# Channel attention with a squared-ReLU FFN: the folded weights of batches 1 to 3 by seven block products, and two steps of batch 0 in another order

## The chip, the cores and the metric

One core of a Trainium2 chip. The time is device microseconds of one launch; "before" is the median of 3 runs. The matrix engine TensorE is PE in the profile (PEld its weight loads), VectorE is DVE, ScalarE is ACT, and SP issues the DMAs.

## The reference

B = 4 batches of N = 6080 tokens with C = 256 channels; w_in is 256x2048, w_out 2048x256.

```
qn = q / (norm(q, axis=1) + 1e-06);  kn = k / (norm(k, axis=1) + 1e-06)
s = kn.transpose(0, 2, 1) @ qn / tau          # 256 x 256 per batch
a = softmax(s)                                # rows
x = v @ a
h = max(x @ w_in, 0)
out = (h * h) @ w_out
```

## The kernel before

v @ a @ w_in is computed as v @ W with W = a w_in, made once per batch: `e` is exp(s) (transposed: eT), `rinv` one over its row sums, and W(b, g) is group g of four, 512 columns of w_in each. Every operand of a product is split in two float32r parts, hi and lo, and a product is three terms: hi hi, hi lo, lo hi.

The tokens of a batch go in 12 blocks (ten of 512, the last two of 480). A **step** is one block and one f of 16 (128 columns of W). In a step PE makes `ps_h` = W v (`first_product`, six matmuls of a block's width), ACT puts relu of it into `x`. Two steps are a **pair**: ACT squares x, DVE makes the sums of the block products (`x<-x`, one op of 512 and two of 256 that depend on each other), ACT casts `g_hi`, DVE subtracts `g_lo`, once over three slots (768 columns) and once over four (1024). Two pairs later PE uses them in `second_product`, seven block products in place of eight, 9 matmuls of 256 in the even step and 12 in the odd (`seven_products`; the first two blocks use `eight_products`, six matmuls of 512 in each step). So in each step PE first makes ps_h, then ps_o, and the ps_o part needs g_hi and g_lo of a pair that ACT and DVE have had some four steps for.

PE, DVE and ACT run in the order in which the program is written; only SP's order is a scheduler's. Work beside the steps sits in generators: `beside` advances by one yield per step, and `attention(b)` (the Gram of q and k of the next batch, its norms, its softmax in `softmax_and_W`) runs beside the blocks of batch b-1. The norms are refined in three rounds of small DVE ops (nx, ny, ns, nu), end in `nr`, and ACT's `s<-gram,nr` waits for nr. At the end of `softmax_and_W` the four W(b, g) are made, in the last block of the batch before: g = 0 at f = 4 and 6, g = 1 at 9 and 11, g = 2 at 14 and the next block's 0, g = 3 at 5 and 7. Each is two halves h of six matmuls of 512 (`ps_w`), each followed a step later by an eviction: ACT writes w_hi (512), DVE w_lo (512, scalar_tensor_tensor from PSUM). The parts of w_in are kept in DRAM (`wi_kept`) and reloaded for each W(b, g).

Batch 0 differs: steps 0 to 31 go through its first two blocks in turn, while DVE and ACT still decode w_in and w_out (`decode`, the tiles dec_e, dec_m, w_raw) and split v (`split_v_hi`, `split_v_lo`). W(0, 1..3) are made in steps 6, 14 and 22 (`steps_of_W`).

Of the kernel before, what the change touches and what calls it, by code (L numbers as in the profile page):

```python
# [8 lines left out]
F32 = mybir.dt.float32  # L9
F32R = mybir.dt.float32r  # L10
# [3 lines left out]
AF = mybir.ActivationFunctionType  # L14
ALU = mybir.AluOpType
# [15 lines left out]
def kernel(  # L31
# [208 lines left out]
    QK_BUFS = 2  # L240
# [134 lines left out]
    def attention(b):  # L375

        if b not in grams:
            grams[b] = Gram(b)
        g = grams[b]
        c0 = HEAD if b == 1 else 0  # L380
        for c in range(c0, min(c0 + QK_BUFS, g.n)):
            g.load(c)
        yield
        for c in range(c0, g.n):
            yield from until_even()
            p, jn, _ = g.q[c]
            hi = pool.tile([P, 2, J, C], F32R, tag="qk_hi", name=f"qk_hi{b}_{c}", bufs=1)
            lo = pool.tile([P, 2, J, C], F32R, tag="qk_lo", name=f"qk_lo{b}_{c}", bufs=1)
            h_, l_, r_ = (x[:p, :, :jn, :] for x in (hi, lo, g.raws[c]))
            scalar.copy(h_, r_)  # L390
            vector.tensor_sub(l_, r_, h_.bitcast(F32))
            yield
            yield from until_even()
            g.squares(c)
            g.add_squares(c)
            if c + QK_BUFS < g.n:
                g.load(c + QK_BUFS)
            for _ in g.products(c, [(hi, hi), (hi, lo), (lo, hi)]):
                yield
        yield from softmax_and_W(b)  # L400

    def pause(b, first, other):

        for _ in range(other if b else first):
            yield

    def softmax_and_W(b):
        gram, acc = grams[b].gram, grams[b].acc
        wi = {0: reload_w_in(b, 0)} if b else {}

        vector.tensor_add(acc[:, :, 0, :], acc[:, :, 0, :], acc[:, :, 1, :])
        yield from pause(b, 1, 2)
# [1 line left out]
        for m in range(2 * NC):  # L414
# [4 lines left out]
                start=m == 0,  # L419
# [5 lines left out]
        x = small("nx")  # L425
# [59 lines left out]
        vector.tensor_copy(eT_hi, ps_tv)  # L485
        vector.tensor_sub(eT_lo, ps_tv, eT_hi.bitcast(F32))
        yield from pause(b, 2, 3)

        for g in range(NG):
            while (b, g) not in may_write_W:  # L490
                yield
            if b == 0:
                while g not in wi_first:
                    yield
                hi, lo = wi_first.pop(g)
                keep_w_in(g, (hi, lo))
# [31 lines left out]

            if b == 0:
                for h, terms in ((0, (0, 1)), (1, (0,)), (0, (2,)), (1, (1, 2))):  # L530
                    products(h, terms)
                yield
                for h in range(NC):
                    evict(h)
            else:
                for h in range(NC):
                    products(h)
                    if h == NC - 1 and g + 1 < NG:
                        wi[g + 1] = reload_w_in(b, g + 1)
                    yield  # L540
                    evict(h)
                    yield
# [291 lines left out]
    for i in range(len(steps) + 2 * LAG):  # L834
        part = now["part"] = i % 2
        if i < len(steps):
            b, n, f = steps[i]
            at = b * NB + n
            first_product(b, n, f)
            if n == NB - 1 and f % FPG == FPG - 1:  # L840
                may_write_W.add((b + 1, f // FPG))

        if i >= PAIR:
            gens = (beside,)
        else:
# [67 lines left out]
```

## Time and profile before

| | |
|---|---|
| median of 3 runs | 2214.52 us (2214.35 to 2214.86) |
| profiled execution | 2215.23 us, span 2213.5 us |
| busy: PE, ACT, DVE | 2205.0, 1847.7, 1774.4 us |
| granted TensorE clock | 1.0 |

PE is busy from end to end, so the time is the sum of PE's matmul pitches plus what PE waits. The durations of PE's rows are longer than the pitch, because a matmul starts before the one ahead of it has ended: what a matmul costs is the distance of starts.

### The profile page before, as it was taken

Reading aid. Unit: us, or ns where it says so; the run is one execution under the profiler, and the core shown is the slowest. Engines: PE = TensorE matmul, PEld = TensorE weight load, DVE = VectorE, ACT = ScalarE, POOL = GpSimd, SP = SyncE. Lnnn points to the kernel's source line nnn. Section 1 sums busy time; section 2 is a strip of 40 time slices with the busy share of each in tenths; the row PEclk is TensorE's granted clock in tenths of the full one; section 3 lists DMA queues with packets and bytes.
Section 4 is the critical chain, followed back from the end, with each engine's and each line's share of the span. In section 5 each row is a group of like instructions: output and inputs, shape, how many; then the busy total and the mean of one; then the engine's idle time right before and its main releaser. Section 6 shows DMA issues by size and latency. Waiting matters only on the chain.

```text
span 2213.5 us, 34513 instructions
## 1 busy us (share of the span) xinstructions
PE 2205.0 (100%) x13795; PEld 1982.1 (90%) x13795; DVE 1774.4 (80%) x2496; ACT 1847.7 (83%) x2300; POOL 0.7 (0%) x6
## 2 busy tenths in 40 slices
PE   9999999999999999999999999999999999999999
PEld 8788999989989999988998999998899888888898
DVE  6878888888778888878767888887877777787786
ACT  5788888888788888888878888888887888888887
POOL 0000000000000000000000000000000000000000
PEclk9999999999999999999999999999999999999999
DMA  9521122101121122110121222110102010010000
GB/s 340 181 77 38 60 74 68 46 19 38 57 67 58 61 69 65 61 41 22 36 76 48 63 68 72 58 53 22 35 23 76 21 37 20 22 36 20 21 27 18
DMA packets 76496, 127.01 MB, mean 57 GB/s; under 512 B 7728, under 2 KB 35120, under 8 KB 76336
## 3 DMA queue, kind: packets, MB, share of 16 engines
q1 hardware_dynamic: 76336, 124.81, 17.4%
q8 instruction: 108, 1.77, 0.3%
q14 instruction: 52, 0.43, 0.1%
HBM read 95.68 MB, written 29.10 MB: 56 GB/s over the span
## 4 chain that ended last, share of the span: by engine, by line
PE 96%; DMA 2%; DVE 1%; ACT 1%; SPq 0%; issue 0%; DVEq 0%; ACTq 0%
PE ps_h L27 47%; PE ps_o L27 42%; PE gram L27 4%; PE ps_w L27 2%; DMA qk<-in_k 1%; DMA qk<-in_q 0%; DVE dec_m L27 0%; DMA qk_heads<-in_q 0%; DMA w_raw<-in_w_in 0%; ACT x L27 0%; ACT g_hi L27 0%; SPq L268 0%; SPq L267 0%; DVE g_lo L27 0%; DVE wi_lo L27 0%
## 5 line engine op out<-in xcount | busy, mean ns | idle before, releaser
L27 DVE TENSOR_TENSOR g_lo<-x,g_hi 128x768 fp32r<-128x768 f32 (+2 forms) x749 | 808.8, 1080 | 78.9 <-ACT g_hi L27 78.2
L27 DVE TENSOR_TENSOR x<-x 128x512 f32<-128x512 f32 (+1 forms) x1095 | 558.4, 510 | 279.5 <-ACT x L27 253.8
L27 ACT CAST g_hi<-x 128x768 fp32r<-128x768 f32 (+2 forms) x749 | 701.8, 937 | 25.3 <-DVE x L27 12.3
L27 ACT ACTIVATE x<-ps_h 128x512 f32<-128x512 f32 (+1 forms) x768 | 455.8, 593 | 282.2 <-PE ps_h L27 264.1
L27 PE MATMUL ps_h<-v_hi,w_hi 128*128 128x512 f32 (+1 forms) x1536 | 478.4, 393 | 0.0
L27 PE MATMUL ps_h<-v_hi,w_lo 128*128 128x512 f32 (+1 forms) x1536 | 477.9, 392 | 0.0
L27 PE MATMUL ps_h<-v_lo,w_hi 128*128 128x512 f32 (+1 forms) x1536 | 475.0, 390 | 0.7 <-DVE v_lo L27 0.7
L27 ACT ACTIVATE x<-x 128x1024 f32<-128x1024 f32 (+1 forms) x384 | 404.5, 1053 | 11.9
L27 PE MATMUL ps_o<-g_lo,wS_hi 128*128 128x256 f32 (+1 forms) x1460 | 407.4, 279 | 0.0
L27 PE MATMUL ps_o<-g_hi,wS_lo 128*128 128x256 f32 (+1 forms) x1460 | 406.6, 279 | 0.0
L27 PE MATMUL ps_o<-g_hi,wS_hi 128*128 128x256 f32 (+1 forms) x1460 | 405.9, 278 | 0.0
L27 PEld LDWEIGHTS ps_h<-v_lo,w_hi 128*128 128x128 f32 x1536 | 287.8, 187 | 65.9 <-DVE v_lo L27 1.2
L27 PEld LDWEIGHTS ps_h<-v_hi,w_lo 128*128 128x128 f32 x1536 | 288.5, 188 | 62.4 <-DVE w_lo L27 0.3
L27 PE MATMUL ps_o<-g_hi,wo_hi 128*128 128x256 f32 (+2 forms) x1159 | 325.2, 285 | 0.0
L27 PE MATMUL ps_o<-g_hi,wo_lo 128*128 128x256 f32 (+2 forms) x1159 | 325.1, 285 | 0.0
L27 PE MATMUL ps_o<-g_lo,wo_hi 128*128 128x256 f32 (+2 forms) x1159 | 324.9, 285 | 0.0
L27 PEld LDWEIGHTS ps_o<-g_lo,wS_hi 128*128 128x128 f32 x1460 | 274.8, 188 | 16.1 <-DVE g_lo L27 0.2
L27 PEld LDWEIGHTS ps_o<-g_hi,wS_hi 128*128 128x128 f32 x1460 | 274.1, 188 | 15.6
L27 PEld LDWEIGHTS ps_o<-g_hi,wS_lo 128*128 128x128 f32 x1460 | 274.4, 188 | 0.0
L27 PEld LDWEIGHTS ps_h<-v_hi,w_hi 128*128 128x128 f32 x1536 | 238.2, 188 | 4.7
L27 PEld LDWEIGHTS ps_o<-g_hi,wo_hi 128*128 128x128 f32 x1159 | 218.4, 188 | 15.6
L27 PEld LDWEIGHTS ps_o<-g_lo,wo_hi 128*128 128x128 f32 x1159 | 217.7, 188 | 15.7 <-DVE g_lo L27 0.3
(96 smaller groups left out, 1689.2 us busy)
## 6 DMA issues: line engine op xcount, KB each, us to landing
qk<-in_k SPq DMA_DIRECT2D x87, 256.0 KB, 2.7
qk<-in_q SPq DMA_DIRECT2D x87, 256.0 KB, 3.0
v<-in_vT SPq DMA_DIRECT2D x40, 512.0 KB, 3.7
out_T<-o SPq DMA_DIRECT2D x152, 128.0 KB, 1.7
wi_hi<-wi_kept SPq DMA_DIRECT2D x12, 512.0 KB, 3.3
wi_lo<-wi_kept SPq DMA_DIRECT2D x12, 512.0 KB, 4.1
w_raw<-in_w_in SPq DMA_DIRECT2D x4, 1024.0 KB, 6.1
w_raw<-in_w_out SPq DMA_DIRECT2D x4, 1024.0 KB, 5.3
```

The costliest lines, as they stand in the source:

```text
L27: return lambda *args, **kwargs: self.tc.keep_in_program_order(issue(*args, **kwargs))
```

## The change

**W of batches 1 to 3.** The two halves by two halves of the product e w_in, twelve matmuls of 512, become seven block products of three terms, 21 matmuls of 256. Four go first (12 matmuls, into `one`, the bank of the Gram, and `two`, a ps_h buffer); ACT copies 256 columns, DVE makes three sums of 256 that depend on each other and adds one of them onto `two` (512 columns); two yields later the other three (9 matmuls), the first of S4 with B22, into `two`. The eviction is four pieces of 256 on ACT and on DVE, in place of two of 512. It stands in the yields where the second half's stood.

**Sums.** T1 to T4, sums of blocks of w_in, are made once, beside batch 1's softmax: `beside_another` lets `sums_of_w_in` go on in two of every five yields. For each g DVE adds hi and lo (1024), makes the sums (512, 256, 256) and subtracts the cast (1024); ACT casts (1024). They are stored in DRAM (`wS_kept`) and reloaded for each W(b, g). S1 to S4, sums of blocks of e, are made in each batch: DVE 512, four of 128 and 512, ACT 512.

**Batch 0.** In step 1 `split_v_lo` of block 1 stands ahead of the weights' stages. In steps 6, 14, 22 the last four matmuls of W, those with wi_lo, and the eviction stand behind that step's second product.

```
+    def sums_of_w_in(b, wi):
...
+            vector.tensor_add(w, hi.bitcast(F32), lo.bitcast(F32))
+            wi[(g + 1) % NG] = reload_w_in(b, (g + 1) % NG)
+            yield
...
+            vector.tensor_sub(S[:, 0:3:2, :], w[:, :, half:], w[:, 0, :].rearrange("p (k t) -> p k t", k=2))
+            vector.tensor_sub(S[:, 1, :], w[:, 1, half:], S[:, 0, :])
+            vector.tensor_sub(S[:, 3, :], w[:, 1, 0:half], S[:, 1, :])
+            yield
+            parts = wi_sums_tiles(b, 0, f"made{g}")
+            scalar.copy(parts[0], S)
+            yield
+            vector.tensor_sub(parts[1], S, parts[0].bitcast(F32))
+            for kept, part in zip(wS_kept[g], parts):
+                nc.sync.dma_start(kept, part.bitcast(F32))
+            yield
+        sums_made.append(b)
...
+        for k, _ in enumerate(main):
+            if k % 5 in (0, 2):
+                next(side, None)
+            yield
...
+            vector.tensor_add(e32, eT_hi.bitcast(F32), eT_lo.bitcast(F32))
...
+            vector.tensor_add(S[:, 0], A21, A22)
+            vector.tensor_sub(S[:, 2], A11, A21)
+            vector.tensor_sub(S[:, 1], S[:, 0], A11)
+            vector.tensor_sub(S[:, 3], A12, S[:, 1])
...
+            while not sums_made:
+                yield
+            wS = {g: reload_sums(b, g) for g in range(2)}
...
+                early = ((0, (0, 1)), (1, (0,)), (0, (2,)), (1, (1, 2))) if g == 0 else ((0, (0, 1)), (1, (0, 1)))
...
+                if g:
+                    for h in range(NC):
+                        products(h, (2,))
                 for h in range(NC):
                     evict(h)
             else:
-                for h in range(NC):
-                    products(h)
...
+                product(one[:, 0], "A11", "B11", start=True)
+                product(one[:, 1], "S2", "T2", stop=True)
+                product(two[:, 0], "S1", "T1", start=True)
+                product(two[:, 1], "S3", "T3")
+                scalar.copy(x[:, 0], one[:, 0])
+                vector.tensor_add(x[:, 1], one[:, 1], x[:, 0])
+                vector.tensor_add(x[:, 2], two[:, 0], x[:, 1])
+                vector.tensor_add(x[:, 3], two[:, 1], x[:, 2])
+                vector.tensor_add(two, two, x[:, 1:2, :].broadcast_to([P, 2, half]))
+                yield
+                yield
+                product(one[:, 0], "A12", "B21", stop=True)
+                product(two[:, 0], "S4", "B22")
+                product(two[:, 1], "A22", "T4", stop=True)
...
             for item in stages.get(i, ()):
                 weights.stage(item)
-            if i == 1:
-                split_v_lo(*order[1])
...
-        if i in steps_of_W:
-            next(first)
...
         if i >= 2 * LAG:
             second_product(*pairs[i // 2 - LAG], part)
+        if i in steps_of_W:
+            next(first)
```

DVE in block 11 of batch 0, while W(1, 0) is evicted and W(1, 1) made; before (behind g_lo and x stand block and pair, behind ps_w group and half):

```order
L27 TENSOR_TENSOR v_lo_0_5542<-v_0_5116,v_hi_0_5488 128x1024 [waits DMAHW1_49]
L27 TENSOR_TENSOR x_11_4_5529<-x_11_4_5529 128x480 [waits Activation_49]
L27 TENSOR_TENSOR x_11_4_5529<-x_11_4_5529 128x240 [waits DVE_49] x2
L27 TENSOR_TENSOR g_lo_11_4_5555<-x_11_4_5529,g_hi_11_4_5554 128x720 [waits Activation_49]
L27 TENSOR_TENSOR o_10_5364<-o_10_5364 128x240
L27 TENSOR_TENSOR o_10_5364<-o_10_5364 128x2x240 [waits DVE_49]
L27 SCALAR_TENSOR_TENSOR w_lo_1_5581<-ps_w_1_0_5582,rinv_4678,w_hi_1_5580 128x512 [waits Activation_49]
L27 TENSOR_TENSOR g_lo_11_4_5555<-x_11_4_5529,g_hi_11_4_5554 128x960 [waits Activation_49]
```

The same stretch now:

```order
L27 TENSOR_TENSOR v_lo_0_5654<-v_0_5191,v_hi_0_5594 128x1024 [waits DMAHW4_49]
L27 TENSOR_TENSOR x_11_4_5641<-x_11_4_5641 128x480 [waits Activation_49]
L27 TENSOR_TENSOR x_11_4_5641<-x_11_4_5641 128x240 [waits DVE_49] x2
L27 TENSOR_TENSOR g_lo_11_4_5667<-x_11_4_5641,g_hi_11_4_5666 128x720 [waits Activation_49]
L27 TENSOR_TENSOR o_10_5453<-o_10_5453 128x240
L27 TENSOR_TENSOR o_10_5453<-o_10_5453 128x2x240 [waits DVE_49]
L27 TENSOR_TENSOR w_sums_1_5696<-ps_w_1_0_5694,w_sums_1_5696 128x256 [waits Activation_49]
L27 TENSOR_TENSOR w_sums_1_5696<-ps_w_1_1_5695,w_sums_1_5696 128x256 [waits DVE_49,PE_49]
L27 TENSOR_TENSOR w_sums_1_5696<-ps_w_1_1_5695,w_sums_1_5696 128x256 [waits DVE_49]
L27 TENSOR_TENSOR ps_w_1_1_5695<-ps_w_1_1_5695,w_sums_1_5696 128x512 [waits DVE_49]
L27 TENSOR_TENSOR g_lo_11_4_5667<-x_11_4_5641,g_hi_11_4_5666 128x960 [waits Activation_49]
```

The w_lo of W(1, 1)'s first half has gone from here (it follows a pair on, with the second half's, as four of 256; just ahead of these rows the w_lo of W(1, 0), one of 512 before, is four of 256 too). In its place stand three sums that follow one another and the addition onto `two`.

PE at the end of step (11, 11), the second set of products of W(1, 1), now:

```order
L27 MATMUL ps_w_1_0_5694<-wi_lo_1_5576,eT_hi_4735 128x256
L27 MATMUL ps_w_1_0_5694<-wi_hi_1_5575,eT_lo_4736 128x256
L27 MATMUL ps_w_1_1_5695<-wi_hi_1_5575,eS_4900 128x256 [waits DVE_49]
L27 MATMUL ps_w_1_1_5695<-wi_lo_1_5576,eS_4900 128x256
L27 MATMUL ps_w_1_1_5695<-wi_hi_1_5575,eS_4900 128x256
L27 MATMUL ps_w_1_1_5695<-wiS_1_1_5390,eT_hi_4735 128x256
L27 MATMUL ps_w_1_1_5695<-wiS_1_1_5391,eT_hi_4735 128x256
L27 MATMUL ps_w_1_1_5695<-wiS_1_1_5390,eT_lo_4736 128x256
```

The third row, S4 with B22, waits for DVE; before, six matmuls of 512 stood here and had no row of DVE to wait for in their own group.

DVE in batch 1's norms, before:

```order
L27 SCALAR_TENSOR_TENSOR nu_4193<-ns_4192,ny_4189 128x4 [waits DVE_49]
L27 SCALAR_TENSOR_TENSOR ny_4189<-nu_4193,ny_4189 128x4 [waits DVE_49]
L27 TENSOR_TENSOR g_lo_8_2_4165<-x_8_2_4142,g_hi_8_2_4164 128x1024 [waits Activation_49]
L27 TENSOR_TENSOR x_8_3_4201<-x_8_3_4201 128x512 [waits Activation_49]
L27 TENSOR_TENSOR x_8_3_4201<-x_8_3_4201 128x256 [waits DVE_49] x2
L27 TENSOR_TENSOR g_lo_8_3_4228<-x_8_3_4201,g_hi_8_3_4227 128x768 [waits Activation_49]
L27 TENSOR_TENSOR o_7_4104<-o_7_4104 128x256
L27 TENSOR_TENSOR o_7_4104<-o_7_4104 128x256 [waits DVE_49]
L27 TENSOR_TENSOR ns_4192<-nx_4186,ny_4189 128x4
```

And now:

```order
L27 SCALAR_TENSOR_TENSOR nu_4207<-ns_4206,ny_4203 128x4 [waits DVE_49]
L27 SCALAR_TENSOR_TENSOR ny_4203<-nu_4207,ny_4203 128x4 [waits DVE_49]
L27 TENSOR_TENSOR wi_sums_4220<-wi_raw_4092 128x2x256
L27 TENSOR_TENSOR wi_sums_4220<-wi_raw_4092,wi_sums_4220 128x256 [waits DVE_49] x2
L27 TENSOR_TENSOR g_lo_8_2_4179<-x_8_2_4156,g_hi_8_2_4178 128x1024 [waits Activation_49]
L27 TENSOR_TENSOR x_8_3_4215<-x_8_3_4215 128x512 [waits Activation_49]
L27 TENSOR_TENSOR x_8_3_4215<-x_8_3_4215 128x256 [waits DVE_49] x2
L27 TENSOR_TENSOR g_lo_8_3_4246<-x_8_3_4215,g_hi_8_3_4245 128x768 [waits Activation_49]
L27 TENSOR_TENSOR o_7_4118<-o_7_4118 128x256
```

The sums of w_in, an op of 512 and two of 256, have come between the first round of the norms and g_lo; all that follows on DVE, the other rounds and nr among it, stands behind them.

## Rows read from the trace of the kernel before

**Rows 1.** The page's part 1 (busy time, share, instructions) and part 4 (the chain of work that ended last, by engine).

```profile
PE 2205.0 (100%) x13795; PEld 1982.1 (90%) x13795; DVE 1774.4 (80%) x2496; ACT 1847.7 (83%) x2300; POOL 0.7 (0%) x6
...
PE 96%; DMA 2%; DVE 1%; ACT 1%; SPq 0%; issue 0%; DVEq 0%; ACTq 0%
```

**Rows 2.** PE's timeline in a step away from W: start, duration, instruction, count. Six matmuls of 512, twelve of 256, and the next step's first.

```profile
1002.07 0.62 PE L27 MATMUL ps_h<-v_hi,w_hi 128*128 128x512 f32 x2
...
1003.46 0.28 PE L27 MATMUL ps_o<-g_hi,wS_hi 128*128 128x256 f32 x1
...
1004.86 0.63 PE L27 MATMUL ps_h<-v_hi,w_hi 128*128 128x512 f32 x2
```

**Rows 3.** PE's timeline in block 11 of batch 0: the first matmuls of the first half of W(1, 1) and of what follows it, and the same of the second half.

```profile
589.69 0.63 PE L27 MATMUL ps_w<-wi_hi,eT_hi 128*128 128x512 f32 x2
...
591.09 0.60 PE L27 MATMUL ps_h<-v_hi,w_hi 128*128 128x480 f32 x2
...
596.05 0.63 PE L27 MATMUL ps_w<-wi_hi,eT_hi 128*128 128x512 f32 x2
...
597.44 0.60 PE L27 MATMUL ps_h<-v_hi,w_hi 128*128 128x480 f32 x2
```

**Rows 4.** The page's part 5, PE's weight loads for ps_o: count, busy time, mean ns.

```profile
L27 PEld LDWEIGHTS ps_o<-g_lo,wS_hi 128*128 128x128 f32 x1460 | 274.8, 188 | 16.1 <-DVE g_lo L27 0.2
```

**Rows 5.** PE's timeline in step 6 of batch 0: W(0, 1), with what it waited for.

```profile
79.44 0.63 PE L27 MATMUL ps_w<-wi_hi,eT_hi 128*128 128x512 f32 x2
80.61 0.73 PE L27 MATMUL ps_w<-wi_lo,eT_hi 128*128 128x512 f32 x2 [0.54 <-DVE wi_lo L27]
81.18 0.63 PE L27 MATMUL ps_w<-wi_hi,eT_lo 128*128 128x512 f32 x2
```

**Rows 6.** DVE's timeline in the same stretch.

```profile
79.34 1.22 DVE L27 TENSOR_TENSOR wi_lo<-dec_m,wi_hi 128x1024 fp32r<-128x1024 f32 x1
```

**Rows 7.** PE's timeline in step 1 of batch 0 and the second product behind it.

```profile
70.09 0.73 PE L27 MATMUL ps_h<-v_lo,w_hi 128*128 128x512 f32 x2 [0.73 <-DVE v_lo L27]
...
73.80 0.72 PE L27 MATMUL ps_o<-g_lo,wo_hi 128*128 128x512 f32 x2
```

**Rows 8.** DVE's timeline of that stretch.

```profile
67.67 1.23 DVE L27 TENSOR_TENSOR wo_lo<-dec_m,wo_hi 128x1024 fp32r<-128x1024 f32 x1
68.82 1.22 DVE L27 TENSOR_TENSOR v_lo<-v,v_hi 128x1024 fp32r<-128x1024 f32 x1
...
72.52 1.23 DVE L27 TENSOR_TENSOR g_lo<-x,g_hi 128x1024 fp32r<-128x1024 f32 x1 [1.34 <-ACT g_hi L27]
```

**Rows 9.** ACT's timeline of that stretch.

```profile
66.58 1.06 ACT L27 CAST wo_hi<-dec_m 128x1024 fp32r<-128x1024 f32 x1 [1.24 <-DVE dec_m L27]
...
71.44 1.04 ACT L27 CAST g_hi<-x 128x1024 fp32r<-128x1024 f32 x1
```

**Rows 10.** DVE's timeline in block 11 of batch 0 (idle time and releaser in brackets).

```profile
585.22 1.55 DVE L27 TENSOR_TENSOR x<-x 128x480 f32<-128x480 f32 x3 [1.68 <-ACT x L27]
...
587.51 0.84 DVE L27 TENSOR_TENSOR o<-o 128x240 f32<-128x240 f32 x2
588.27 0.74 DVE L27 SCALAR_TENSOR_TENSOR w_lo<-ps_w,rinv,w_hi 128x512 fp32r<-128x512 f32 x1
...
594.41 0.74 DVE L27 SCALAR_TENSOR_TENSOR w_lo<-ps_w,rinv,w_hi 128x512 fp32r<-128x512 f32 x1
595.08 1.15 DVE L27 TENSOR_TENSOR g_lo<-x,g_hi 128x960 fp32r<-128x960 f32 x1
```

**Rows 11.** DVE's timeline in batch 1's norms.

```profile
453.64 1.61 DVE L27 TENSOR_TENSOR x<-x 128x512 f32<-128x512 f32 x3 [0.81 <-ACT x L27]
...
457.63 0.16 DVE L27 SCALAR_TENSOR_TENSOR ny<-nu,ny 128x4 f32<-128x4 f32 x1
457.71 1.22 DVE L27 TENSOR_TENSOR g_lo<-x,g_hi 128x1024 fp32r<-128x1024 f32 x1
...
469.54 0.18 DVE L27 RECIPROCAL nr<-ns 128x4 f32<-128x4 f32 x1
...
471.56 1.23 DVE L27 TENSOR_TENSOR g_lo<-x,g_hi 128x1024 fp32r<-128x1024 f32 x1 [1.32 <-ACT g_hi L27]
```

**Rows 12.** ACT's timeline behind the norms.

```profile
469.75 0.84 ACT L27 ACTIVATE s<-gram,nr 128x256 f32<-128x256 f32 x2 [3.98 <-DVE nr L27]
470.48 1.05 ACT L27 CAST g_hi<-x 128x1024 fp32r<-128x1024 f32 x1
```

**Rows 13.** PE's timeline there.

```profile
472.65 0.28 PE L27 MATMUL ps_o<-g_hi,wS_hi 128*128 128x256 f32 x1
472.83 0.39 PE L27 MATMUL ps_o<-g_lo,wS_hi 128*128 128x256 f32 x1
```

**Rows 14.** Busy time of each engine in windows: PE, PEld, DVE, ACT, POOL (x instructions), granted clock, DMA share, GB/s.

```profile
473.14:517.55 44.41, 44.41 (x284) 39.93 (x283) 38.27 (x57) 38.94 (x52) 0.00 (x0) 1.00 0.08 24
```

**Rows 15.** DVE's timeline behind the norms.

```profile
491.65 1.61 DVE L27 TENSOR_TENSOR x<-x 128x512 f32<-128x512 f32 x3 [1.06 <-ACT x L27]
...
515.95 1.23 DVE L27 TENSOR_TENSOR g_lo<-x,g_hi 128x1024 fp32r<-128x1024 f32 x1 [0.25 <-ACT g_hi L27]
```

**Rows 16.** PE's timeline in step (9, 15): the first product with the g_lo that rows 15 show last.

```profile
520.98 0.28 PE L27 MATMUL ps_o<-g_lo,wS_hi 128*128 128x256 f32 x1
```

**Rows 17.** The page's part 6, DMA issues: KB each, us from issue to landing.

```profile
wi_lo<-wi_kept SPq DMA_DIRECT2D x12, 512.0 KB, 4.1
```

More of the change, by code (lines that the diff above doesn't have):

```diff
@@ L151 @@
     wi_kept = [[scratch.tile([P, NC, GRP], F32, name=f"wi_kept{g}_{i}") for i in range(2)] for g in range(NG)]
+    wS_kept = [[scratch.tile([P, 4, GRP // 2], F32, name=f"wi_sums_kept{g}_{i}") for i in range(2)] for g in range(NG)]
     def wi_tiles(b, g):
@@ L232, in reload_w_in, with beside_another, wi_sums_tiles, reload_sums @@
         for kept, part in zip(wi_kept[g], parts):
+            nc.sync.dma_start(part.bitcast(F32), kept)
+        return parts
+    def sums_of_w_in(b, wi):
+        half = GRP // 2
+        wi[0] = reload_w_in(b, 0)
+        yield
+        for g in range(NG):
+            hi, lo = wi.pop(g)
+            w = pool.tile([P, NC, GRP], F32, tag="qk", name=f"wi_raw{g}", bufs=QK_BUFS)
+            vector.tensor_add(w, hi.bitcast(F32), lo.bitcast(F32))
+            wi[(g + 1) % NG] = reload_w_in(b, (g + 1) % NG)
+            yield
+            S = pool.tile([P, 4, half], F32, tag="qk", name=f"wi_sums{g}", bufs=QK_BUFS)
+            vector.tensor_sub(S[:, 0:3:2, :], w[:, :, half:], w[:, 0, :].rearrange("p (k t) -> p k t", k=2))
[10 more added lines that the diff above has]
+        sums_made.append(b)
+    sums_made = []
+    def beside_another(main, side):
+        for k, _ in enumerate(main):
+            if k % 5 in (0, 2):
+                next(side, None)
+            yield
+    def wi_sums_tiles(b, i, name):
+        at = (dict(tag="qk_hi", bufs=1), dict(tag="qk_lo", bufs=1)) if i == 0 else (dict(tag="qk", bufs=QK_BUFS),) * 2
+        return [pool.tile([P, 4, GRP // 2], F32R, name=f"wiS{p}_{b}_{name}", **a) for p, a in enumerate(at)]
+    def reload_sums(b, g):
+        parts = wi_sums_tiles(b, g % 2, f"{g}")
+        for kept, part in zip(wS_kept[g], parts):
             nc.sync.dma_start(part.bitcast(F32), kept)
@@ L399, in attention @@
                 yield
-        yield from softmax_and_W(b)
+        if b == 1:
+            wi = {}
+            yield from beside_another(softmax_and_W(b, wi), sums_of_w_in(b, wi))
+        else:
+            yield from softmax_and_W(b, {0: reload_w_in(b, 0)})
     def pause(b, first, other):
@@ L405, in pause, with softmax_and_W @@
             yield
-    def softmax_and_W(b):
+    def softmax_and_W(b, wi=None):
         gram, acc = grams[b].gram, grams[b].acc
-        wi = {0: reload_w_in(b, 0)} if b else {}
         vector.tensor_add(acc[:, :, 0, :], acc[:, :, 0, :], acc[:, :, 1, :])
@@ L487, in softmax_and_W @@
         yield from pause(b, 2, 3)
+        if b:
+            room = pool.tile([P, 2, NC * C], F32, tag="acc", name=f"e_sums{b}", bufs=1)
+            e32, S = room[:, 0].rearrange("p (d c) -> p d c", d=NC), room[:, 1].rearrange("p (s c) -> p s c", s=4)
+            vector.tensor_add(e32, eT_hi.bitcast(F32), eT_lo.bitcast(F32))
+            yield
+            (A11, A12), (A21, A22) = [[e32[:, j, i * P : (i + 1) * P] for j in range(2)] for i in range(2)]
+            vector.tensor_add(S[:, 0], A21, A22)
[3 more added lines that the diff above has]
+            yield
+            eS = pool.tile([P, 2, 4, P], F32R, tag="dec", name=f"eS{b}", bufs=1)
+            scalar.copy(eS[:, 0], S)
+            yield
+            vector.tensor_sub(eS[:, 1], S, eS[:, 0].bitcast(F32))
+            yield
+            while not sums_made:
+                yield
+            wS = {g: reload_sums(b, g) for g in range(2)}
         for g in range(NG):
@@ L529, in softmax_and_W @@
             if b == 0:
-                for h, terms in ((0, (0, 1)), (1, (0,)), (0, (2,)), (1, (1, 2))):
+                early = ((0, (0, 1)), (1, (0,)), (0, (2,)), (1, (1, 2))) if g == 0 else ((0, (0, 1)), (1, (0, 1)))
+                for h, terms in early:
                     products(h, terms)
                 yield
+                if g:
+                    for h in range(NC):
+                        products(h, (2,))
                 for h in range(NC):
@@ L535, in softmax_and_W @@
             else:
-                for h in range(NC):
-                    products(h)
[L538 to L542, printed above, removed]
+                half = GRP // 2
+                Ts = wS.pop(g)
+                A = {f"A{i + 1}{j + 1}": [e[:, j, i * P : (i + 1) * P] for e in (eT_hi, eT_lo)] for i in range(2) for j in range(2)}
+                A.update({f"S{i + 1}": [eS[:, p, i] for p in range(2)] for i in range(4)})
@@ new lines, in softmax_and_W, with product @@
+                D = {f"B{j + 1}{k + 1}": [w[:, j, k * half : (k + 1) * half] for w in (hi, lo)] for j in range(2) for k in range(2)}
+                D.update({f"T{i + 1}": [p[:, i, :] for p in Ts] for i in range(4)})
+                def product(ps, a, d, start=False, stop=False):
+                    for i, (x, y) in enumerate(((0, 0), (0, 1), (1, 0))):
+                        tensor.matmul(ps, A[a][x], D[d][y], start=start and i == 0, stop=stop and i == 2, skip_group_check=True)
+                one = ps_g.tile([P, NC, C], F32, tag="gram", name=f"ps_w{b}_{g}_0")
@@ new lines, in softmax_and_W @@
+                two = ps_h.tile([P, T], F32, tag="h", name=f"ps_w{b}_{g}_1").rearrange("p (k t) -> p k t", k=2)
+                x = pool.tile([P, 4, half], F32, tag="acc", name=f"w_sums{b}_{g}", bufs=1)
+                product(one[:, 0], "A11", "B11", start=True)
[4 more added lines that the diff above has]
+                vector.tensor_add(x[:, 1], one[:, 1], x[:, 0])
@@ new lines, in softmax_and_W @@
+                vector.tensor_add(x[:, 2], two[:, 0], x[:, 1])
+                vector.tensor_add(x[:, 3], two[:, 1], x[:, 2])
+                vector.tensor_add(two, two, x[:, 1:2, :].broadcast_to([P, 2, half]))
+                yield
+                yield
+                product(one[:, 0], "A12", "B21", stop=True)
+                product(two[:, 0], "S4", "B22")
+                product(two[:, 1], "A22", "T4", stop=True)
+                if g + 1 < NG:
+                    wi[g + 1] = reload_w_in(b, g + 1)
@@ new lines, in softmax_and_W @@
+                if g + 2 < NG:
+                    wS[g + 2] = reload_sums(b, g + 2)
+                yield
+                for h, k, src in ((0, 0, one[:, 0]), (0, 1, two[:, 0]), (1, 0, two[:, 1]), (1, 1, x[:, 3])):
+                    at = slice(k * half, (k + 1) * half)
+                    scalar.activation(w_hi[:, h, at], src, AF.Copy, scale=rinv[:, h : h + 1])
+                    vector.scalar_tensor_tensor(
+                        w_lo[:, h, at],
+                        src,
+                        rinv[:, h : h + 1],
+                        w_hi[:, h, at].bitcast(F32),
+                        op0=ALU.mult,
+                        op1=ALU.subtract,
+                    )
@@ L543, in softmax_and_W @@
+                yield
             W[b, g] = w_hi, w_lo
@@ L845 @@
         else:
+            if i == 1:
+                split_v_lo(*order[1])
             for item in stages.get(i, ()):
                 weights.stage(item)
-            if i == 1:
-                split_v_lo(*order[1])
             gens = (first,) if i in steps_of_W else ()
```

## The prediction

> **What bounds the kernel now.** I read the page first: PE is busy for 2205.0 of 2213.5 us and makes 96% of the chain of waits; DVE (80%) and ACT (83%) have room on average [rows 1]. So an edit gains what it takes from PE's matmuls or from PE's waits, and loses what it makes PE wait, and the second is a matter of place: wherever g_lo is ready just in time, every microsecond put in front of it on DVE is a microsecond of PE. So PE's and DVE's timelines come next, at the four places that the change touches.
>
> **W by seven products: what PE gains.** In a step away from W six matmuls of 512 take 1003.46 - 1002.07 = 1.39 us (232 ns each) and twelve of 256 take 1.40 (117 ns each) [rows 2]. A half of W is six of 512: 591.09 - 589.69 = 1.40, and 597.44 - 596.05 = 1.39 [rows 3], so 2.79 for each g. Now it is 21 of 256: 21 x 0.117 = 2.45. Saved: 0.34 for each g, in 4 groups of 3 batches, 12 x 0.34 = **-4.1 us**. With 121 ns for one of 256, 3% more than the row, it would be 0.25 and -3.0; with 116, 0.35 and -4.3.
>
> The rows speak on a rule against this edit. A load of weights takes 188 ns on average [rows 4], yet the twelve of 256, each with its own load, follow at 117 ns: loads lie beside matmuls, and the smaller shape costs no more per column. The Trainium skill, "TensorE: Matmul & The Clock Gate", section "Back-to-back issue gap", gives a sustained spacing of 81 ns for 128 columns and 131 ns for 512 in a stream of loads and matmuls. An estimate between them, about 98 for 256, would give 21 x 98 = 2.06 against 12 x 131 = 1.57 us, a loss of 0.49 a group or 5.9 in all. The trace disagrees with both spacings (232 and 117 ns, one to two), and the measurement decides.
>
> **W: the wait that it adds.** The three sums and the addition onto `two` have to end before S4 with B22. For g = 1 they stand late. Before, DVE starts x<-x at 585.22 and is never idle until 596.2 [rows 10]. Now PE, and with it ACT's square, comes 0.34 earlier, as the second set of g = 0 is 9 x 0.117 = 1.05 and not 1.39: DVE starts at 584.9. The four w_lo of 256 cost 4 x 0.40 in place of 0.66 (dependent ops of 240 take 0.42 each by the pair of o, 0.84 for two [rows 10]; no row has this op at 256, and between half of 0.66 and 0.42 I take 0.40): +0.94. The sums then start where w_lo stood, 594.41 - 0.34 + 0.94 = 595.0, and take 3 x 0.42 + 0.75 = 2.0: 597.0. PE comes to S4 at 596.05 - 0.34 + 0.35 (A12 with B21) = 596.06. It waits about 1.0, and some 0.1 for the semaphores between: 1.05 in each batch, since DVE's order is the same in each, **+3.2 us** (0.5 to 1.6 in each: +1.5 to +4.8). Queued behind it on PE is all of the next step. In the other three groups the sums end 1.4 us or more ahead by the same walk, and I take nothing. ACT's casts in four pieces of 256 stand in its idle time (it waits for PE several times in this stretch). `two` holds one of three ps_h buffers for two steps more; ACT reads ps_h within a us of its last matmul and a step is over 2.3, so two are enough.
>
> Reloads: a 512 KB part lands in 4.1 us [rows 17]; the sums of w_in for g = 0 and 1 are asked for a block ahead and those of g + 2 with the second set, a step and more than 5 us ahead of their use, on queues that are busy for 8% [rows 14]. They cost nothing; were the cover gone, the price would be the rest of 4.1 us.
>
> **The sums of w_in in batch 1's softmax.** This is the large cost. DVE runs from 453.64 with no idle time until nr at 469.54 is done [rows 11]; ACT's s<-gram waited 3.98 us for nr, g_hi stands behind that, g_lo behind g_hi (471.56 to 472.79), and PE's first product with g_lo, due 0.12 after 472.65, starts at 472.83 [rows 11 to 13]: the margin is nothing. The order now puts three ops between 457.63 and 457.71, of the shape of x<-x x3 (1.61, 1.5 by pitch [rows 11]). All of it comes out 1.5 later, so PE waits **1.5**, with no cover.
>
> From there DVE has more to do until the last g_lo of block 9's pair 5 (515.95): two casts' remainders and two raw sums at 1.14 (a 1024 by pitch), two more triples at 1.5, sums of e 0.6 + 4 x 0.25 + 0.1 = 1.7, in all 4 x 1.14 + 3.0 + 1.7 = 9.3. In that window DVE is busy for 38.3 of 44.4 us [rows 14], so 6.1 are idle, and at its end g_lo (ended 517.1 [rows 15]) is used at 520.98 [rows 16]: a margin of 3.9. If all idle time could be used, DVE would come out 1.5 + 9.3 - 6.1 - 3.9 = 0.8 late, under the 1.5 that is lost already; if none, 6.9. A walk pair by pair comes near the upper end: the pairs with additions have 0.3 to 0.8 idle each, and the largest idle stretch (1.06 before 491.65 [rows 15] and those next to it) lies in pairs that get no DVE op but a cast on ACT (0.95), which is what they wait for. Used idle time is about 1.4: I take **+5.5 us** (1.5 to 6.9). Behind 517.55 the rest (cast's remainder, group 3) meets more idle time and no narrow margin. Batches 2 and 3 get only the sums of e, 1.7 and 0.6, in pairs with a margin of the size of this 3.9: nothing. The stores and the reloads of w_in go by SP's queue ahead of q, k and v with some us to spare: nothing, a loss at most of one landing.
>
> **Batch 0.** In step 6 PE is at wi_lo 0.71 us late (80.61, from 79.44 + 2 x 0.23 = 79.90), as DVE's wi_lo ends at 80.56, and two matmuls then take 0.57 in place of 0.47 [rows 5, 6]: 0.8. The six matmuls of second product that now stand ahead (1.4 us) cover it: **-0.8** (0 to -0.8). The later eviction is covered by ACT, which comes to it after 82. Steps 14 and 22 show no wait and get none.
>
> In step 1 PE is idle for 0.73 at v_lo [rows 7]; with a restart as slow as step 6's and the gap in starts I put the wait at 1.0. v_lo now takes wo_lo's place at 67.67 and ends at 68.9, ahead of PE. But the second product needs g_lo, which ended at 73.75 with PE at 73.80 [rows 7, 8], and g_lo waits for ACT's g_hi at 71.44, at the end of a chain on ACT that runs unbroken from 66.58 [rows 9] and does not move. So PE only waits there: **0** (0 to -1.0).
>
> **Sum**, against the profiled execution: -4.1 + 3.2 + 5.5 - 0.8 + 0 = +3.8, and 2215.2 + 3.8 = 2219.0 us. The median of the runs is 0.7 lower, so I give 2218.3. What can be told from no change with this kernel is 0.2%, 4.4 us: under 2210.1 is faster, over 2218.9 slower. The forecast stands at the edge of that.
>
> **Rivals.**
> (a) DVE's added work hides, because it flows into idle time better than a walk in fixed order says, and the sums of W end in time: -4.1 - 0.8 + 0.5 (what is left at nr) = -4.4, 2210.1. For it: DVE idle for 6.1 us in the window. Against it: DVE without idle time ahead of nr and of S4, 1.5 and 1.0 us that no other work covers. With one of the two waits gone it is 2211 to 2214, inside no change. Chance of faster 0.10.
> (b) Slower: DVE in blocks 8 and 9. ACT's two casts of 0.95 add to the cycle DVE x<-x, ACT g_hi, relu, square, x<-x, and the loss there reaches 6.9, with S4's wait at 1.3 in each batch: -4.9 + 6.9 + 3.9 = +5.9, 2220.4. It decides from a loss of over 6.1 in those blocks (with S4 as forecast). For it: the walk is near the upper end. Chance 0.38.
> (c) The products of 256 don't come at half the price: from 2.79 / 21 = 133 ns each the edit gains nothing, and at a load's 188 ns it loses 1.16 a group, 13.9 in all: 2236. Row against it: 117 ns. The Trainium skill's rule above is the case for it. Chance 0.02, counted with slower.
>
> **How the numbers follow.** Forecast with smaller losses, 2211 to 2218.9: 0.50, the likeliest value at its upper end. Slower with (b) and (c) 0.40, faster 0.10. The range takes in the lower ends (1.5 for the softmax, 1.5 for S4: -4.9 + 3.0 = -1.9, 2212.6) and (b) with S4 at 1.6, 2221.3: 2212.0 to 2221.3.
>
> **What would show it.** In the profile after: W's 21 matmuls of 256 at 117 ns, 2.45 a group (right) or over 133 (c). PE idle 1.0 ahead of the first ps_w with eS in the second set of g = 1, releaser DVE, in all three batches, or no idle time (then the sums start before 594.7 of the old clock). PE idle 1.5 at the first g_lo of the step (8, 13), and more waits for g_lo in steps (9, 9) to (9, 15); without them (a) is right. PE without the 0.54 at wi_lo in step 6; the wait of step 1 gone from v_lo and come again at the g_lo behind it. I am wrong if PE's waits are elsewhere: at reloaded sums, in batches 2 and 3's softmax, or in groups 0, 2 and 3.

## The result, and the profile after

| | before | changed |
|---|---|---|
| median (6 runs each) | 2214.34 us | 2230.15 us (2228.9 to 2234.0) |
| span of the profiled execution | 2213.5 us | 2227.5 us |

The ratio is 1.0073, 95% interval 1.0062 to 1.0083: 15.8 us slower, where 2218.3 (2212.0 to 2221.3) had been forecast. The sign of the sum was right, its size was not.

Page after, parts 1 and 4, to be held against [rows 1]:

```profile
PE 2208.1 (99%) x13903; PEld 1986.0 (89%) x13903; DVE 1819.7 (82%) x2606; ACT 1858.0 (83%) x2343; POOL 0.7 (0%) x6
...
PE 89%; DVE 5%; ACT 3%; DMA 2%; issue 0%; SPq 0%; ACTq 0%; DVEq 0%
```

PE's share of the chain fell from 96% to 89%; DVE and ACT now hold 8% of it. PE's waits after (released by; total us, times, longest):

```profile
PE ps_w L27 <- DVE w_sums L27: 3.4, 3, 1.1
PE ps_w L27 <- DVE ps_w L27: 3.3, 3, 1.1
PE ps_o L27 <- ACT o L27: 3.2, 8, 0.7
PE ps_o L27 <- DVE g_lo L27: 3.1, 4, 1.2
```

Before, no wait of PE for any of these four was on the list. Where the time went is found by comparing, step by step, the start of the first ps_h matmul of a step in both traces, counted from step (0, 0) on (a step is named by its block and f):

| stage | forecast | measured |
|---|---|---|
| batch 0, first two blocks | -0.8 | -0.7 |
| blocks 8 and 9 of batch 0 (sums of w_in) | +5.5 | +6.0 |
| W of batches 1 to 3: PE's matmuls | -4.1 | -3.4 (taken from the run below without waits) |
| W of batches 1 to 3: PE's waits | +3.2 | 10.1 + 3.4 = +13.5 (1.4 of it a lower clock behind the waits of batch 1, last section) |
| sum | +3.8 | +15.4 |

(The spans differ by 14.0, since the profiled execution of before waited 1.0 longer for its first loads, and its last step was 0.3 longer.) So three terms held and one was over 10 us too small. This is how that one looks. ACT in block 11 of batch 0 before, where neither w_hi waits for DVE:

```profile
585.92 0.68 ACT L27 ACTIVATE w_hi<-ps_w,rinv 128x512 fp32r<-128x512 f32 x1
...
593.05 0.68 ACT L27 ACTIVATE w_hi<-ps_w,rinv 128x512 fp32r<-128x512 f32 x1
```

ACT there now, in the eviction of W(1, 0):

```profile
589.92 0.83 ACT L27 ACTIVATE w_hi<-ps_w,rinv 128x256 fp32r<-128x256 f32 x2
593.16 0.47 ACT L27 ACTIVATE w_hi<-ps_w,rinv 128x256 fp32r<-128x256 f32 x1 [2.42 <-DVE w_lo L27]
...
593.94 0.56 ACT L27 ACTIVATE x<-ps_h 128x480 f32<-128x480 f32 x1
594.39 0.99 ACT L27 CAST g_hi<-x 128x960 fp32r<-128x960 f32 x1
```

and DVE there, the stretch of [rows 10]:

```profile
592.26 0.87 DVE L27 SCALAR_TENSOR_TENSOR w_lo<-ps_w,rinv,w_hi 128x256 fp32r<-128x256 f32 x2
593.67 0.49 DVE L27 SCALAR_TENSOR_TENSOR w_lo<-ps_w,rinv,w_hi 128x256 fp32r<-128x256 f32 x1 [0.54 <-ACT w_hi L27]
...
595.41 1.16 DVE L27 TENSOR_TENSOR g_lo<-x,g_hi 128x960 fp32r<-128x960 f32 x1 [0.86 <-ACT g_hi L27]
...
600.91 1.41 DVE L27 TENSOR_TENSOR w_sums<-ps_w,w_sums 128x256 f32<-128x256 f32 x3
602.35 0.70 DVE L27 TENSOR_TENSOR ps_w<-ps_w,w_sums 128x512 f32<-128x512 f32 x1
```

ACT's third w_hi starts 0.03 after DVE's second w_lo ends (593.13), and ACT was idle for 2.42 ahead of it. Behind it stand ACT's x and g_hi, behind g_hi DVE's g_lo (0.86 idle), behind that, on DVE, the sums of W(1, 1) and the addition onto `two`, which ends at 603.05. PE, which needs them:

```profile
601.38 0.38 PE L27 MATMUL ps_w<-wi_hi,eT_hi 128*128 128x256 f32 x1 [1.13 <-DVE w_sums L27]
...
603.10 0.58 PE L27 MATMUL ps_w<-wi_hi,eS 128*128 128x256 f32 x1 [1.10 <-DVE ps_w L27]
603.48 0.41 PE L27 MATMUL ps_w<-wi_lo,eS 128*128 128x256 f32 x1
603.69 0.41 PE L27 MATMUL ps_w<-wi_hi,eS 128*128 128x256 f32 x1
```

PE waits twice: 1.13 at A12 with B21, which writes `one`, for the first of the sums, which reads `one`, and 1.10 at S4 with B22 for the addition onto `two`. Then it runs at 210 ns a matmul of 256. The same ACT wait comes in the eviction of W(1, 2), in the next block, where it makes the copies of ps_o late and PE waits for those. ACT's timeline:

```profile
626.71 0.47 ACT L27 ACTIVATE w_hi<-ps_w,rinv 128x256 fp32r<-128x256 f32 x1 [1.73 <-DVE w_lo L27]
...
628.89 0.77 ACT L27 COPY o<-ps_o 128x720 f32<-128x720 f32 x1
```

PE's timeline there:

```profile
629.71 0.39 PE L27 MATMUL ps_o<-g_hi,wo_hi 128*128 128x256 f32 x1 [0.18 <-ACT o L27]
...
633.03 0.39 PE L27 MATMUL ps_o<-g_hi,wS_hi 128*128 128x256 f32 x1 [0.59 <-ACT o L27]
```

Behind the norms, against [rows 11, 13]: the wait that was forecast at the first g_lo behind nr is there. DVE's timeline:

```profile
456.00 0.69 DVE L27 TENSOR_TENSOR wi_sums<-wi_raw 128x512 f32<-128x512 f32 x1
456.72 0.88 DVE L27 TENSOR_TENSOR wi_sums<-wi_raw,wi_sums 128x256 f32<-128x256 f32 x2
...
471.30 1.23 DVE L27 TENSOR_TENSOR g_lo<-x,g_hi 128x1024 fp32r<-128x1024 f32 x1 [1.32 <-ACT g_hi L27]
```

PE's timeline there:

```profile
472.58 0.38 PE L27 MATMUL ps_o<-g_lo,wS_hi 128*128 128x256 f32 x1 [0.88 <-DVE g_lo L27]
```

Step (8, 13) is 1.46 longer. Batch 0, PE against [rows 5, 7]: there is no wait for wi_lo any more, and the one for v_lo has become one for g_hi.

```profile
71.53 0.73 PE L27 MATMUL ps_o<-g_hi,wo_hi 128*128 128x512 f32 x2 [0.56 <-ACT g_hi L27]
...
80.78 1.10 PE L27 MATMUL ps_w<-wi_lo,eT_hi 128*128 128x512 f32 x4
```

### The profile page after: what moved, and what is told of

Its sections match the earlier page's. It is cut to its first block, busy times and chain, and to the rows that moved or that the text cites. A ratio compares the mean times of both kernels' runs of the same rounds, so it can differ in the third digit from the quotient of the medians.

```text
span 2227.5 us, 34975 instructions
## 1 busy us (share of the span) xinstructions
PE 2208.1 (99%) x13903; PEld 1986.0 (89%) x13903; DVE 1819.7 (82%) x2606; ACT 1858.0 (83%) x2343; POOL 0.7 (0%) x6
## 4 chain that ended last, share of the span: by engine, by line
PE 89%; DVE 5%; ACT 3%; DMA 2%; issue 0%; SPq 0%; ACTq 0%; DVEq 0%
PE ps_h L27 44%; PE ps_o L27 39%; PE gram L27 4%; PE ps_w L27 2%; DVE x L27 1%; DVE g_lo L27 1%; ACT x L27 1%; DMA qk<-in_k 1%; DVE o L27 0%; ACT g_hi L27 0%; DMA qk<-in_q 0%; DVE v_lo L27 0%; ACT o L27 0%; DMA qk_heads<-in_q 0%; DVE w_lo L27 0%
```

## The experiments

Times are medians with their ratio to the kernel before, run on the same chip. The last three columns are the step comparison of above by stage, from each run's profiled execution, in us against the kernel before (Gram: blocks 2 to 7 of batch 0; C: blocks 8 to 10 of batch 0; E: W of the three later batches together, with what PE's matmuls save there).

| run | us | ratio (95%) | Gram | C | E |
|---|---|---|---|---|---|
| changed | 2230.15 | 1.0073 (1.0062 to 1.0083) | 0 | 6.0 | 10.1 |
| e1_evict_order | 2219.70 | 1.0025 (1.0015 to 1.0034) | 0 | 6.0 | 0.1 |
| e2_sums_unused | 2217.94 | 1.0016 (1.0007 to 1.0025) | 0 | 4.5 | 0 |
| e3_batch0_only | 2213.67 | 0.9996 (0.9987 to 1.0006) | 0 | 0 | 0 |
| e4_sums_after_nr | 2234.36 | 1.0089 (1.0074 to 1.0104) | 0 | 10.1 | 11.7 |
| e5_sums_on_pool | 2228.96 | 1.0071 (1.0054 to 1.0088) | 0 | 15.5 | 0.3 |
| e6_one_step_more | 2217.10 | 1.0012 (1.0003 to 1.0022) | 0 | 5.9 | -3.4 |
| e7_pool_and_step | 2225.46 | 1.0051 (1.0036 to 1.0066) | 0 | 15.5 | -3.4 |
| e8_pool_e_sums | 2228.40 | 1.0064 (1.0049 to 1.0079) | 0 | 18.0 | -3.4 |
| e9_sums_in_gram | 2212.01 | 0.9988 (0.9979 to 0.9997) | 1.7 | 0 | -3.4 |
| e10_third_from_sbuf | 2227.30, one run | - | 0 | 6.0 | 7.9 |
| e11_step_alone | 2224.71, one run | - | 0 | 6.0 | 4.8 |
| e12_sums_off_crowd | 2215.68 | 1.0003 (0.9994 to 1.0012) | 5.2 | 0 | -3.4 |
| e13_behind_qk_lo | 2210.17 | 0.9982 (0.9973 to 0.9991) | 0 | 0 | -3.4 |

**Theory A against rival B: whose wait is late in W?** In e1 ACT makes its four w_hi first, and DVE its four w_lo after them.

```
-                for h, k, src in (...):
-                    scalar.activation(w_hi[:, h, at], src, ...)
-                    vector.scalar_tensor_tensor(w_lo[:, h, at], src, ...)
+                pieces = (...)
+                for h, k, src in pieces:
+                    scalar.activation(w_hi[:, h, at], src, ...)
+                for h, k, src in pieces:
+                    vector.scalar_tensor_tensor(w_lo[:, h, at], src, ...)
```

> The changed kernel, but in the eviction of W(b, g) ACT gets its four w_hi first and DVE its four w_lo after them (the same eight instructions, in another order). Theory A: the third w_hi reads the PSUM bank `two` which DVE's second w_lo reads too, and so had to wait for it (2.42 us idle on ACT in g = 1's stage, 1.73 in g = 3's); that delayed g_hi, g_lo, the sums of the next group and the copy of ps_o. Then the wait goes, the net loss at the second set of g = 1 falls from 2.4 us a batch to about 0.7 (the wait of 1.05 that was forecast, less the 0.35 saved), the 1.3 us in steps 5 and 6 of the next block vanish, and the kernel comes out about 10 us faster than the changed one, near 2219 to 2220. Rival B: it is DVE's added work alone (3 us a group) that is late; then the order of the eviction matters for less than 2 us, 2228 to 2230.

2219.70: the same eight instructions in another order are worth 10.4 us. ACT runs through:

```profile
589.81 1.20 ACT L27 ACTIVATE w_hi<-ps_w,rinv 128x256 fp32r<-128x256 f32 x3
590.89 0.52 ACT L27 ACTIVATE w_hi<-w_sums,rinv 128x256 fp32r<-128x256 f32 x1
```

Of PE's waits for ps_w only S4's is left, 2.7 in three (from the steps, with the 0.34 added back that the nine matmuls save, 0.85 + 0.34 = 1.2 a batch, where 1.05 had been forecast), and the waits in the next block are gone. A holds and B falls. Whether it is what the piece reads, or its place as the third, e10 tests, with the third and the fourth exchanged:

```
-... (0, 1, two[:, 0]), (1, 0, two[:, 1]), (1, 1, x[:, 3]) ...
+... (0, 1, two[:, 0]), (1, 1, x[:, 3]), (1, 0, two[:, 1]) ...
```

> The changed kernel with the third and the fourth piece of the eviction exchanged: the third w_hi reads w_sums (SBUF), the fourth reads the second half of `two`. Theory A (the wait comes from the PSUM bank that DVE's second w_lo reads): now the third does not wait for DVE's w_lo and the fourth does, for about as long (2.4 us of ACT's idle time in g = 1's stage less one piece), and the time stays at the changed kernel's, 2227 to 2231. Rival: the third waits whatever it reads (a limit of two pieces in flight on w_hi's buffer): the wait stays at the third.

The third, from SBUF, follows at once, and the fourth waits. ACT's timeline in batch 2's W, and DVE's:

```profile
1139.34 0.51 ACT L27 ACTIVATE w_hi<-w_sums,rinv 128x256 fp32r<-128x256 f32 x1
1141.87 0.47 ACT L27 ACTIVATE w_hi<-ps_w,rinv 128x256 fp32r<-128x256 f32 x1 [2.02 <-DVE w_lo L27]
...
1140.96 0.87 DVE L27 SCALAR_TENSOR_TENSOR w_lo<-ps_w,rinv,w_hi 128x256 fp32r<-128x256 f32 x2
```

The fourth starts 0.04 after DVE's second w_lo, which reads `two`, has ended (1141.83). So ACT's read of one half of `two` waits for DVE's read of the other half. The Trainium skill states such a rule ("PSUM — Partial Sum Buffer", section "PSUM bank collisions raise a hardware error"): the compiler's scheduler adds a dependency between accesses of two engines to the same PSUM bank and partitions, two reads as well. The trace agrees, with waits of 2.42 and 2.02 us. No run tells the bank from the tile `two` as what the wait hangs on. In the kernel before each half of W had a tile of its own.

**One step more in g = 1.** `for _ in range(3 if g == 1 else 2): yield` ahead of the second set, with the new eviction order (e6) and without (e11).

> The kernel of the eviction in another order, with one yield more between the two sets of products of g = 1 (so g = 2 and 3 come one step later too); the sums stay on DVE. Theory: the 1.2 us that PE still waits at S4 with B22 in each batch is the end of the sums on DVE; a step (2.3 us) later it is over: -3.6 in all, 2216.1. Rival: the wait moves with the products (what DVE has in front moves too) or comes back at g = 2 or 3: 2218.5 or more.

> The changed kernel with the yield more in g = 1 alone; the eviction as in the changed kernel, with its wait. Theory: the step hides 2.3 of the 2.8 us at S4 in each batch, and the 1.7 us gross in steps 5 and 6 of the next block, which come from the same wait of ACT in the eviction, stay or move with it: 2221 to 2224. Rival: the eviction's wait only acts through S4; then the step hides nearly all of it: 2217 to 2218.

With both, all of W's waits go: -3.4 in E, which is what PE's matmuls give. In e11 (one run, 0.7 over the theory's range) E stays at +4.8, 1.6 a batch: the step hides part of S4's wait, not the eviction's. e6's 2217.10 is 1.0 over the expectation, 0.7 of it because W's matmuls give 3.4 and not 4.1: in the trace after, the first twelve of W(1, 1) take from 593.68 to 595.12, 120 ns each.

**The sums of w_in.**

> The changed kernel with W of the later batches by the six products of the kernel before; the sums of w_in are still made and stored beside batch 1's softmax, and not used; the sums of e are left out. Theory: the loss of 6.1 us in blocks 8 and 9 of batch 0 is DVE's (and ACT's) work on the sums, of which 1.7 + 0.6 on DVE (sums of e) are missing here: +4 to +4.5 there, -0.8 in batch 0, nothing elsewhere: 2217.5 to 2218. Rival: the loss in those blocks needs the reloads and W's stage too (queues, the PSUM bank); then it is under 1.5 here and the kernel comes out at 2213.5 to 2215.

4.5 us in blocks 8 and 9 with W as before: it is the work on the sums that costs there. The 1.5 that are missing to 6.0 go with the sums of e, which are left out: step (9, 15), 1.47 longer in the changed kernel, is not longer here.

```
-            if k % 5 in (0, 2):
+            if k >= 10 and k % 5 in (0, 2, 4):
                 next(side, None)
```

> The changed kernel, with the sums of w_in begun ten yields later (behind nr) and then in three of five yields, so that none of them stands between the rounds of the norms; as much work in all. Theory: the 1.46 us at the first g_lo behind nr go, the rest meets the same narrow margins: the loss in blocks 8 and 9 falls from 6.1 to about 4.5 and the kernel gains 1 to 2 us on the changed one (2228 to 2229). Rival: what counts is only the total of DVE's work up to block 9's end, and the loss stays at 6 or more (2230 or more).

This went against me: nr's wait of 1.46 is gone, but the work, packed closer, costs 6.3 in blocks 8 and 9 and 3.8 more in block 10. E is 1.6 larger than in the changed kernel, 1.3 of it in batch 3, where the granted clock fell as in the last section (0.66 in the mean from 1706 to 1711). Neither rate nor total alone decides; each place has its own room.

**GpSimd in place of DVE** (`pool_engine.tensor_add` and `tensor_sub` in `sums_of_w_in`; e8: for the sums of e too).

> The kernel of the eviction in another order (ACT's four, then DVE's four), with the additions and subtractions that make the sums of w_in on GpSimd (POOL) in place of DVE; ACT's casts and the sums of e stay. Theory: the 6.0 us in blocks 8 and 9 are DVE's work in front of g_lo, not the casts and not the DMAs: with that work on the idle POOL what is left is the sums of e (1.7 us, against a margin of 3.9) and the casts, 0 to 1 us; 2213.7 to 2215. Rival: POOL's ops hold up DVE's where they run at once, or come so late that the casts and the reloads are late: 2217 or more.

> Both together: the sums of w_in on POOL and one yield more in g = 1. If the two costs are independent: 2214.4 - 0.7 - 4.1 + 0 to 1 = 2209.6 to 2210.6, under the kernel before. If one hides the other: 2212 or more.

> As the kernel with both, and the sums of e on POOL too, in each batch. If the sums of e still cost PE something in batch 1 (up to 1 us), it goes: 2209.6. If POOL is slow enough to make W late, or works against DVE: 2211 or more.

The theory's number failed in all three, by 14 us in e5, 15 in e7 and 19 in e8: C is 15.5, 15.5 and 18.0. DVE's timeline in the norms, an op of the kernel before first, then two of e5:

```profile
462.10 0.15 DVE L27 TENSOR_TENSOR ns<-nx,ny 128x4 f32<-128x4 f32 x1
...
459.73 2.96 DVE L27 TENSOR_TENSOR o<-o 128x256 f32<-128x256 f32 x2
462.62 2.35 DVE L27 TENSOR_TENSOR ns<-nx,ny 128x4 f32<-128x4 f32 x1
```

POOL's timeline in e5 there:

```profile
459.98 2.43 POOL L27 TENSOR_TENSOR wiS_made<-wi_sums,wiS_made 128x1024 fp32r<-128x1024 f32 x1 [22.37 <-ACT wiS_made L27]
462.37 2.58 POOL L27 TENSOR_TENSOR wi_raw<-wi_hi,wi_lo 128x1024 f32<-128x1024 f32 x1
```

An op of four columns, 0.15 us before, lasts 2.35, to 464.97, and POOL's op ends at 464.95. The Trainium skill ("SBUF — State Buffer", section "SBUF: two separate sides") says that a DVE op with two SBUF inputs and a GpSimd op that reads SBUF share a port pair, which the one that starts first holds to its end. The trace agrees, 2.35 us in place of 0.15. POOL's ops of 1024 take 2.43 and 2.58, twice DVE's own 1.22, and DVE waits for them. So these runs don't test the theory: what DVE was spared it lost again behind POOL. How much of C is DVE's work and how much ACT's casts, no run shows; the next three move both together. Part of C here is the clock: in e7 the granted clock fell to 0.50 around 471, 512 and 540.

**The same sums at another place.** In e9 a piece goes on behind each chunk of q and k in batch 1's Gram, in the tiles wi_hi, wi_lo and dec; on top of e6.

```
             for _ in g.products(c, [(hi, hi), (hi, lo), (lo, hi)]):
                 yield
+            next(side, None)
...
-            yield from beside_another(softmax_and_W(b, wi), sums_of_w_in(b, wi))
+        yield from softmax_and_W(b, {0: reload_w_in(b, 0)})
```

> The eviction in another order and the yield more in g = 1, and the sums of w_in on DVE again, but made during batch 1's Gram (blocks 2 to 7 of batch 0), one piece of work behind each chunk of q and k, in the tiles wi_hi, wi_lo and dec, which are free there. Same operations in the same number. Theory: the 6 us were a matter of place; in the Gram's blocks DVE is idle for 7 to 8 of 50 us and g_lo has 3 to 4 us to spare, an op of 1.2 to 1.5 every 14 us is hidden: 2214.3 - 0.7 - 4.1 = 2209.5, up to 2210.5 with what the sums of e cost. Rival: DVE's total counts wherever it stands, or the DMAs of 8 MB collide with q and k there: 2213 or more.

The 6 us are gone; 1.7 stand in the Gram, where PE waits for qk_lo behind a piece:

```profile
PE gram L27 <- DVE qk_lo L27: 1.0, 2, 0.7
```

e12 lets a piece go on only outside of steps 5 to 11 of a block; e13 puts it behind the split `qk_lo` of each chunk.

> As the kernel with the sums in the Gram, whose two remaining waits (0.9 in block 4, 0.6 in block 6: PE's Gram products wait for qk_lo, which stood behind a piece of the sums in the steps where DVE also splits v and adds up the block before) should go: a piece goes on only outside of steps 5 to 11 of a block, and stands behind q's and k's squares. Theory: place alone; 1.0 to 1.7 us less than that kernel, 2210.3 to 2211. Rival: the pieces wait for each other elsewhere (before qk_lo at a block's end) and it stays at 2212 or more.

> As the kernel with the sums in the Gram (one piece for each chunk, at the same pace, so that each reload of w_in has a chunk's time to land), but each piece stands behind the split qk_lo of a chunk and not ahead of it. Theory: the 1.7 us that were left there are PE's Gram products waiting for qk_lo behind a piece; with qk_lo first the piece only meets g_lo, which has room: 2210.3 to 2210.8, W's gain of 4.1 and batch 0's 0.7 whole. Rival: the work itself delays the following g_lo or the next qk_lo as much: 2212 or more.

In e12 those two waits went, but pieces that had been held back now followed one another faster than a reload lands. PE waits once for 3.4, and step (7, 0) is 4.8 longer; behind the wait the granted clock was 0.52 from 394.0 to 397.4. PE's wait, and DVE's timeline ahead of it:

```profile
PE gram L27 <- DVE qk_lo L27: 3.4, 1, 3.4
...
391.39 1.23 DVE L27 TENSOR_TENSOR wi_raw<-wi_hi,wi_lo 128x1024 f32<-128x1024 f32 x1 [4.45 <-DMA wi_lo<-wi_kept]
```

e13 keeps the pace, and no wait of the change is left but the one for g_hi in batch 0 (PE's waits, the three largest of the whole run):

```profile
PE ps_first L27 <- DVE exp_bias L27: 1.1, 1, 1.1
PE gram L27 <- DMA qk<-in_q: 0.6, 2, 0.3
PE ps_o L27 <- ACT g_hi L27: 0.6, 1, 0.6
```

2210.17: 4.0 us under the kernel before and 20 under the changed one, -0.7 and -3.4 by stages, with the same operations in the same number. So every loss of the change was one of order or place, and none is bound to its operations.

**Batch 0 alone.**

> The kernel before with the two edits of batch 0 alone (v's split ahead of the weights' stages, the low terms of W behind the second product). Theory: the wait for wi_lo goes (-0.8), the wait for v_lo only moves to g_lo (0): 2213.5. Rival: the wait for v_lo is gained as well: 2212.5.

2213.67, which the medians alone don't tell from no change (the interval takes in 1). By steps it is -0.7, from -0.8 in step 6; nothing is gained in step 1.

## Why the prediction was wrong

- **W's matmuls** (-4.1): right in mechanism, -3.4 in size, inside the bounds of 3.0 to 4.3. The rival by weight loads (c) falls: 117 to 120 ns.
- **The sums beside the softmax** (+5.5): right in size, 6.0, and for the most part in kind: 1.46 of the forecast 1.5 at nr, 3.0 at g_lo in steps (9, 12), (9, 13) and (9, 15). But 1.4 lies in steps (9, 4) and (9, 5), where PE waits for ACT's copies of ps_o, a wait that the prediction didn't walk; that the number came so close is in part luck. The walk pair by pair, not the account of idle time, was the better guide: the bounds had been 1.5 and 6.9.
- **Batch 0** (-0.8 and 0): right, -0.7 and 0; the v_lo wait moved to the second product behind it, as written, though to its g_hi (0.56) and not its g_lo.
- **S4's wait** (+3.2): right in what was walked, as e1 shows (1.2 a batch against 1.05).
- **The step that failed** is the sentence "ACT's casts in four pieces of 256 stand in its idle time". The third piece has to wait for DVE's second w_lo, 2.42 us in the stage of g = 1; I counted the duration of the pieces and not what they wait for, nor who is queued behind them on ACT: x, g_hi, the copies of ps_o. With it falls "I take nothing" for the other three groups. Their sums did end in time, as written (PE's six waits for ps_w all lie in g = 1), but the eviction of W(b, 2) made the copies of ps_o late. Measured, by e1: 10.0 us in the three batches, of which 4.0 in the block behind (0.46 and 0.87 net at f = 4 and 5, three times) and 1.4 the lower clock in batch 1.
- The range was too narrow for the same reason: its bounds were bounds of sizes, and the wait that was left out had none.
- Rival (b), slower, had the right side, but not for its reason: the loss in blocks 8 and 9 was 6.0, not over 6.1. That is luck.

## What to carry to other kernels

Where an eviction is cut into pieces and two engines read them in turn, look at which pieces share a PSUM bank or tile: let one engine read all, then the other, or the pieces go back and forth at the pace of the busier engine. Work that is to hide beside a saturated engine is priced by its place: the sums of w_in, some 15 us of DVE (4 x 3.8), cost 4.5 beside the softmax, 1.7 in the Gram ahead of a split that PE waits for, and nothing behind that split. For each added instruction that waits, ask who stands behind it on its own engine.

## What I had not expected of the hardware

The two waits ahead of the second set in batch 1 cost more than their length. PE's granted clock (window; busy of PE, PEld, DVE, ACT, POOL; clock; DMA share; GB/s):

```profile
598.00:601.00 3.00, 2.25 (x17) 1.94 (x15) 2.90 (x7) 2.23 (x4) 0.00 (x0) 1.00 0.57 173
...
603.00:605.00 2.00, 1.90 (x8) 1.83 (x9) 1.97 (x4) 0.00 (x0) 0.00 (x0) 0.50 0.07 18
...
1152.00:1156.00 4.00, 2.90 (x17) 2.51 (x18) 3.84 (x7) 1.08 (x2) 0.00 (x0) 1.00 0.36 101
```

After PE had been idle for most of 601 to 603 (0.62 busy of 2.00), it was granted 0.50, the lower level of 1.2 GHz, up to about 606, and matmuls of 256 followed at 210 ns in place of 117. In batches 2 and 3, with waits of the same length, the clock stayed at 1.0 (the last line is batch 2) and steps (11, 11) and (11, 12) were together shorter by 1.4 (4.1 over before in batch 1, 2.8 in the others, with the 0.34 that the matmuls save added back). The changed kernel's runs lie 5 us apart (2228.9 to 2234.0), the kernel before's 0.8. The spread goes with the clock: the mean granted clock of the six runs, in the order of their times, was 1.0, 0.999, 0.999, 0.998, 0.998 and 0.997. Why the clock falls behind the same wait in one batch or run and not in another, no run here shows.
